# Tile 2 of the input transposed by a DMA instead of TensorE, with a new order of the first phase's steps

## Chip, cores and metric

One core of a Trainium2 chip. The metric is device time in microseconds (us) of one execution; a smaller number is better. Engines are named as in the profile: PE is TensorE's matmul stream, PEld its weight loads, DVE VectorE, ACT ScalarE, POOL GpSimd, SP the engine that issues most DMAs.

## What is computed

The input x has 2048 rows of 512 (bf16). It is layer-normalised, then goes through a linear-attention block and a gated feed-forward block, whose results are added to x.

```python
xn  = layernorm(x)                                   # no weight, no bias
qkv = xn @ wqkv                                      # 32 heads of 16
pq, pk = phi(q), phi(k)                              # phi(t) = (t+1 if t>0 else exp(t)) + 1e-6
kv  = einsum("bhsd,bhse->bhde", pk, v); z = pk.sum(over rows)
o   = einsum("bhqd,bhde->bhqe", pq, kv) / (einsum("bhqd,bhd->bhq", pq, z) + 1e-6)
out = x + o @ wo + (silu(xn @ w_gate) * (xn @ w_up)) @ w_down      # feed-forward width 1792
```

## The kernel before, in words

The rows are cut into 16 tiles of 128. The kernel has three stages. **Phase 1** (to about 48.7 us of the span) loads x, normalises each tile, transposes it, multiplies it with the query and key columns of wqkv, applies phi, and accumulates G = xn^T pk over all tiles in four PSUM banks. The middle stage makes the gate and up products of the feed-forward block (for rows from 384 on with a seven-product scheme for 2x2 blocks). The last stage makes the down projection and adds the attention part. All engines run their own instruction streams, in order; a small planner (`_Program`, line 63) puts a semaphore wait in front of each instruction that reads or overwrites something another engine has yet to finish. Nothing reorders anything: **the order of phase 1 is a hand-written list of steps** (the string given to `run`, line 536), and each engine executes its own steps in that order.

A step is a letter and a tile number. Those that matter here, with the engine and the line of their code:

- `S`: mean and variance of a tile, two instructions on DVE (L307, L310). `M`: minus the mean of tile 1, on ACT (L334).
- `R`: 1/standard deviation, two small ACT instructions (L314, L316). `r`: three more small ones for tiles 0 and 1 (L321 to L323); `o`: two small POOL instructions that use them (L326, L329).
- `a`, `b`, `C`: tiles 0 and 1, which are only centred before the product (DVE, L339, L349). `L`: normalise a tile on DVE (L377); `P`: the same on POOL, one small instruction and one large (L392, L395); `N`, `A` do it with ACT.
- `J`: the normalised copy of tile 0 or 1 that G needs, on POOL, a small and a large instruction (L369, L372).
- `c`, `d`, `W`, `X`: four 128x128 transposes of a tile on PE into a PSUM bank (L407; `c` and `d` do two each): `W` uses bank 2, `X` bank 3. `e`, `f`, `w`, `Z`: the copy of that bank to SBUF (ACT L415, DVE L417).
- `D`: the other way to transpose: one transposing DMA, issued by SP (L423).
- `K`, `k`: first and second half of the key product of a tile, `Q`, `q` those of the query product (PE, L444; two matmuls of 128x512 a half for tiles 0 to 3; from tile 4 on `k` and `q` are whole, four matmuls).
- `x`, `y`: exp of that product, ACT (L462 for tiles 0 and 1, L465). `z`: a copy of a query product out of its bank, ACT (L454), for tiles whose `u` comes much later.
- `m`, `n`: the minimum in phi, POOL (L472). `s`, `u`: the sum that gives pk or pq, DVE (L483).
- `G`: the four matmuls of a tile for G (PE, L493). `F`: filler matmuls (L297) that only keep PE busy.

A product takes the next of **four PSUM banks, 4 to 7, in turn** (`nextbank`, line 432). It may only overwrite a bank when the ACT and DVE steps (`x` and `s`, or `y` and `u`, or `y` and `z`) of the product four places earlier have read it. So a product waits for work that belongs to another tile, and the order of the products decides which.

Tiles 0 to 3 are transposed by PE, the others by `D`. The loads of x are issued first: the halves of tile 0, tiles 1 and 3, by SP, the second half of tile 0 and tile 2 by ACT; then SP issues three parts of wqkv and, in one run, tiles 4 to 15. The transposing DMAs follow on the same SP stream (first `D5`), and the loads of the feed-forward weights come behind some of them.

Of the kernel before, what the change touches and what calls it, by code (L numbers as in the profile page):

```python
# [121 lines left out]
def bass_parallel_sum__linear_attn_block__swiglu_ffn__prompt_kernel(nc, A_x, A_wqkv, A_wo, B_x, B_w_gate, B_w_up, B_w_down, out):  # L122
# [5 lines left out]
    with contextlib.ExitStack() as es:  # L128
# [401 lines left out]
        def run(text):  # L530
            late = {int(w[1:]) for w in text.split() if w[0] == "z"}
            later.update({t: i for i, t in enumerate(int(w[1:]) for w in text.split() if w[0] == "u" and int(w[1:]) in late)})
            for w in text.split():
                steps[w[0]](int(w[1:]))

        run("""
            S0 M1 a0 b0 c0 R0 d0 F2 C1 S3 e0 N0 W1 r0 K0 o0 f0 R3 w1 S2 K1 P3 k0 S1 R2 J0 W3 x0 k1 Q1 L2 R1 w3
            m0 X2 q1 r1 Z2 Q3 s0 x1 o1 q3 S5 y1 K3 m1 k3 R5 n1 s1 G0 z1 L5 J1 x3 S9 K2 D5 Q0 z3 m3 S4 k2 R9 q0
            y3 P9 s3 G1 x2 S8 R4 m2 D9 Q2 z0 q2 P4 s2 R8 k5 z2 L8 n3 D4 S15 q5 x5 y0 S12 m5 G2 D8 y5 s5 q9 y2
            n5 S10 R15 k9 n0 y9 u5 R12 n9 k4 x9 L15 u9 D15 q4 m9 x4 L12 R10 s9 m4 q8 y4 D12 S11 P10 k8 z8 s4  # L540
            n4 R11 D10 G9 S13 x8 N11 A11 G5 m8 u4 y8 n2 s8 D11 G3 R13 S14 A0 P13 k15 S7 R14 k12 n8 D13 x15 L14
            S6 m15 q10 x12 D14 s15 m12 k10 y10 s12 n10 k11 x10 u10 R7 m10 q15 x11 s10 q11 m11 y15 L7 R6 s11
            D7 n15 k13 y11 u15 q13 n11 x13 L6 u11 D6 m13 q14 y13 s13 n13 q12 y14 u13 n14 k14 y12 u14 n12 q7
            x14 u12 m14 k7 y7 L1 s14 D0 D1 n7 k6 x7 u0 m7 q6 u7 x6 s7 m6 G4 y6 s6 n6 G12 u2 G14 u6 u1 G6 u8 G10
            u3 G11 G15 G8 G13 G7
        """)
        fload("sp", "wg", wg, B_w_gate, 1)
        wload("sp", 2)
# [304 lines left out]
        X1, X2 = slice(T0, T0 + TB), slice(T0 + TB, S)  # L853
# [507 lines left out]
```

## Time and profile before

| | |
|---|---|
| median of 3 runs | 199.21 us (199.07 to 199.49) |
| the profiled execution, its time | 199.49 us |
| its span from first to last instruction | 198.2 us |
| PE busy | 193.8 us (98%) |
| DVE busy | 170.6 us (86%) |
| ACT busy | 157.3 us (79%) |
| POOL busy | 127.6 us (64%) |
| granted TensorE clock | 1.00 |

A timeline row reads: start in us from the span's start, duration in us, engine, line, operation, output<-input, shape, how many instructions the row merges, and in brackets the engine's idle time just before and what ended it. PE rows end late: matmuls are pipelined, so the time that one costs is read from one start to the next, not from the duration. The same holds, by 0.1 us or less, for the other engines. A row of DMA issues gives the size and the median time from issue to landing.

### The profile page before, as it was taken

How to read it: one execution, taken by the hardware profiler on the slowest of the kernel's cores; microseconds unless marked ns; L12 is line 12 of the kernel's file. 1: busy time of each engine (PE TensorE's matmuls, PEld its weight loads, DVE VectorE, ACT ScalarE, POOL GpSimd, SP SyncE). 2: the span in 40 equal slices, each digit the busy share in tenths (PEclk: the TensorE clock that was granted, in tenths of full speed). 3: DMA queues.
4: the chain of work that ended last, by engine and by line, in shares of the span. 5: the costliest groups of instructions: out<-in, count | busy, mean ns of one | idle time of the engine just before them, and what ended most of it. 6: DMA issues, size and time to landing. Idle time of an engine off the chain costs nothing.

```text
span 198.2 us, 3561 instructions
## 1 busy us (share of the span) xinstructions
PE 193.8 (98%) x1193; PEld 115.2 (58%) x1207; DVE 170.6 (86%) x328; ACT 157.3 (79%) x314; POOL 127.6 (64%) x158
## 2 busy tenths in 40 slices
PE   8899999999999999999999999999999999999995
PEld 2344444444655555555555555555555888888884
DVE  2999998896997799887888998887888999998886
ACT  3799888699698998898999888998897967575300
POOL 3687877799999487689778877868579004413220
PEclk9999999999999999999999999999999999999999
DMA  5943248799900000111110221111000012132223
GB/s 171 360 131 81 61 86 231 211 275 373 348 14 0 3 0 0 28 26 30 28 26 2 55 53 26 26 26 31 2 0 2 3 40 66 33 77 66 45 65 121
DMA packets 28899, 15.97 MB, mean 81 GB/s; under 512 B 17232, under 2 KB 28880, under 8 KB 28880
## 3 DMA queue, kind: packets, MB, share of 16 engines
q1 hardware_dynamic: 28320, 15.28, 28.1%
q10 hardware_dynamic: 560, 0.46, 0.7%
q8 instruction: 9, 0.15, 0.3%
q14 instruction: 10, 0.08, 0.1%
HBM read 9.70 MB, written 2.10 MB: 60 GB/s over the span
## 4 chain that ended last, share of the span: by engine, by line
PE 94%; DVE 2%; DMA 2%; issue 1%; ACT 0%; POOL 0%; SPq 0%
PE pb L896 35%; PE pb L1104 16%; PE pb L444 13%; PE pb L565 9%; PE pb L493 7%; PE pb L719 6%; PE pb L1110 5%; DMA x_sb<-in_A_x_dram 2%; PE pb L723 2%; PE pb L625 0%; PE pb L711 0%; DVE pq L483 0%; PE pb L407 0%; POOL ef L472 0%; DVE stats L307 0%
## 5 line engine op out<-in xcount | busy, mean ns | idle before, releaser
L691 POOL TENSOR_TENSOR pq<-pq,rden 128x512 bf16<-128x512 bf16 x16 | 16.9, 1056 | 36.2 <-DVE rden L684 26.7
L896 PE MATMUL pb<-xnT,wgu 128*128 128x416 bf16 x112 | 26.6, 339 | 0.0
L444 PE MATMUL pb<-wqkv,xnT 128*128 128x512 bf16 x110 | 25.1, 379 | 0.2
L665 POOL TENSOR_TENSOR pz<-pq,zbc 128x512 f32<-128x512 bf16 x16 | 18.9, 1180 | 5.1 <-ACT pz L658 3.5
L565 PE MATMUL pb<-xnT,wgu 128*128 128x384 bf16 x112 | 19.9, 326 | 0.1
L931 DVE TENSOR_TENSOR pb<-p,pb 128x416 f32<-128x416 f32 x28 | 16.6, 595 | 3.6 <-PE pb L896 1.9
L472 POOL TENSOR_SCALAR ef<-ef 128x512 bf16<-128x512 bf16 x25 | 15.5, 620 | 5.8 <-ACT ef L465 5.6
L926 ACT ACTIVATE zacc<-pb,iw 128x416 bf16<-128x416 f32 x28 | 16.4, 614 | 3.1 <-PE pb L896 2.3
L444 PEld LDWEIGHTS pb<-wqkv,xnT 128*128 128x128 bf16 x112 | 10.9, 98 | 13.4 <-DVE pk L483 0.4
L936 DVE TENSOR_TENSOR c<-pb,p 128x416 f32<-128x416 f32 x28 | 16.4, 588 | 2.3 <-PE pb L896 0.3
L465 ACT ACTIVATE ef<-pb 128x512 bf16<-128x512 f32 x25 | 14.8, 593 | 3.9 <-PE pb L444 3.9
L940 POOL TENSOR_TENSOR hT<-c,zacc 128x416 bf16<-128x416 f32 x16 | 15.3, 974 | 2.3 <-ACT zacc L926 1.7
L510 POOL TENSOR_TENSOR zacc<-zacc,pk 128x512 f32<-128x512 f32 x13 | 16.0, 1232 | 1.0
L906 ACT ACTIVATE pb<-pb 128x416 f32<-128x416 f32 x28 | 13.7, 501 | 3.0 <-PE pb L896 1.9
L896 PEld LDWEIGHTS pb<-xnT,wgu 128*128 128x128 bf16 x112 | 10.9, 98 | 8.7
L921 ACT ACTIVATE zacc<-pb,iw 128x416 bf16<-128x416 f32 x28 | 15.7, 626 | 0.0
L565 PEld LDWEIGHTS pb<-xnT,wgu 128*128 128x128 bf16 x112 | 10.8, 98 | 7.0 <-DVE xn L613 0.2
L1104 PE MATMUL pb<-wgu,xnT 128*128 128x256 f16 (+1 forms) x112 | 14.9, 273 | 0.0
L896 PE MATMUL pb<-xnT,wqkv 128*128 128x416 bf16 x56 | 14.4, 339 | 0.3
L896 PE MATMUL pb<-wo,wqkv 128*128 128x416 f16 x56 | 14.4, 339 | 0.0
L896 PE MATMUL pb<-GT,wqkv 128*128 128x416 f16 x56 | 14.4, 339 | 0.0
L307 DVE BATCH_NORM_STATS2 stats<-x_sb 128x6 f32<-128x512 bf16 x16 | 10.8, 678 | 3.2 <-DMA x_sb<-in_A_x_dram 3.2
(202 smaller groups left out, 494.1 us busy)
## 6 DMA issues: line engine op xcount, KB each, us to landing
x_sb<-in_A_x_dram SPq DMA_DIRECT2D x14, 128.0 KB, 3.8
wgu<-in_B_w_gate_dram SPq DMA_DIRECT2D x2, 896.0 KB, 5.2
wgu<-in_B_w_up_dram SPq DMA_DIRECT2D x2, 896.0 KB, 8.0
wd<-in_B_w_down_dram SPq DMA_DIRECT2D x2, 896.0 KB, 13.1
out_dram<-out_sb SPq DMA_DIRECT2D x24, 64.0 KB, 1.6
wqkv<-in_A_wqkv_dram SPq DMA_DIRECT2D x3, 256.0 KB, 4.4
wqkv<-in_A_wqkv_dram SPq DMA_DIRECT2D x1, 512.0 KB, 6.3
wo<-in_A_wo_dram SPq DMA_DIRECT2D x1, 512.0 KB, 8.8
```

What stands on the lines that cost most here:

```text
L444: K.add("pe", [(lambda e, c=c: e.matmul(banks[b][:, :], src[:, c, t * P:(t + 1) * P], wqkv[:, c, col:col + D], start=(c == 0), stop=(c == ...
L472: K.add("pool", lambda e: e.tensor_scalar(out=buf, in0=buf, scalar1=top, scalar2=0.0, op0=ALU.min, op1=ALU.max), r=[bkey] + tkeys, w=[bkey])
L510: K.add("pool", lambda e: e.tensor_tensor(out=dst, in0=acc, in1=more, op=ALU.add), r=[key, mkey], w=[dkey])
L565: fns.append(lambda e, c=c, b=b, w_=w_: e.matmul(banks[b][:, 0:T0], w_[:, c, fc * P:(fc + 1) * P], xnT[:, c, 0:T0], start=(c == 0), stop=( ...
L665: K.add("pool", lambda e: e.tensor_tensor(out=halves(i), in0=two(pq[:, t, :]), in1=two(zbc[:, :]), op=ALU.mult), r=[("pq", t), ("zbc",)] + ...
L691: K.add("pool", lambda e: e.tensor_tensor(out=heads(pq[:, t, :]), in0=heads(pq[:, t, :]), in1=rden[:, i, :][:, :, None].broadcast_to([P, N ...
L896: K.add("pe", [(lambda e, c=c: e.matmul(banks[bank][:, 0:TS], L[i][:, c, :], R[i][:, c, ts], start=(start and c == 0), stop=(c == 1), skip ...
L921: K.add("act", lambda e: e.activation(sil4[:, q, :], bk(a), ACT.Silu, scale=iw[:, 0:1]), r=[B(a), ("iw",)], w=[("sil4", q)], a=[("zacc", 0 ...
L926: K.add("act", lambda e: e.activation(sil4[:, 2 + q, :], bk(d), ACT.Silu, scale=iw[:, 0:1]), r=[B(d), ("iw",)], w=[("sil4", 2 + q)], a=[(" ...
L931: K.add("dve", lambda e: e.tensor_tensor(out=bk(d), in0=p5[:, q, :], in1=bk(b), op=ALU.subtract), r=[B(b), ("p5", q)], w=[B(d)])
L936: K.add("dve", lambda e: e.tensor_tensor(out=c22[:, q, :], in0=bk(b), in1=p5[:, q, :], op=ALU.subtract), r=[B(b), ("p5", q)], w=[("c22", q)])
L1104: K.add("pe", [(lambda e, k=k: e.matmul(split(banks[b][:, 0:HD]), L[:, k, :], cut[:, :, k * P:(k + 1) * P], start=(start and k == 0), stop ...
```

## The change

Only the list of steps changes. `X2` and `Z2` (transposes of tile 2 on PE and their copy on DVE) are gone; `D2`, a transposing DMA, takes their place, and is the first on SP, ahead of `D5`. The order of the steps is rewritten from the start to about `G2`; from `k4` on the two lists agree.

```diff
-S0 M1 a0 b0 c0 R0 d0 F2 C1 S3 e0 N0 W1 r0 K0 o0 f0 R3 w1 S2 K1 P3 k0 S1 R2 J0 W3 x0 k1 Q1 L2 R1 w3
-m0 X2 q1 r1 Z2 Q3 s0 x1 o1 q3 S5 y1 K3 m1 k3 R5 n1 s1 G0 z1 L5 J1 x3 S9 K2 D5 Q0 z3 m3 S4 k2 R9 q0
-y3 P9 s3 G1 x2 S8 R4 m2 D9 Q2 z0 q2 P4 s2 R8 k5 z2 L8 n3 D4 S15 q5 x5 y0 S12 m5 G2 D8 y5 s5 q9 y2
-n5 S10 R15 k9 n0 y9 u5 R12 n9 k4 x9 L15 u9 D15 ...
+S0 a0 b0 M1 c0 d0 R0 F2 e0 S2 C1 f0 S3 r0 R3 W1 N0 K0 k0 S1 o0 x0 w1 P3 m0 R2 K1 W3 k1 R1 L2 J0 w3 r1 Q1
+q1 s0 o1 S5 K3 x1 z1 k3 Q3 y1 R5 q3 x3 J1 G0 m1 S9 D2 s1 y3 L5 R9 Q0 K2 S4 S8 z3 m3 k2 R4 x2 D5 P9 G1 s3
+q0 n1 R8 Q2 y0 L8 m2 D9 q2 s2 z0 z2 k5 x5 y2 D8 P4 n0 q5 D4 m5 y5 n3 S10 q9 S15 R15 k9 n5 s5 y9 S12 u5
+G2 n9 R12 L15 u9 k4 x9 D15 ...
```

By engine, the first steps are then (before, after):

```
PE    c0 d0 F2 W1 K0 K1 k0 W3 k1 Q1 X2 q1 Q3 q3 K3 k3 G0 K2 Q0 k2 q0 G1 Q2 q2 k5 q5 G2 q9 k9 | k4
      c0 d0 F2 W1 K0 k0 K1 W3 k1 Q1 q1 K3 k3 Q3 q3 G0 Q0 K2 k2 G1 q0 Q2 q2 k5 q5 q9 k9 G2    | k4
DVE   S0 a0 b0 C1 S3 f0 w1 S2 S1 L2 w3 Z2 s0 S5 s1 L5 S9 S4 s3 S8 s2 L8 S15 S12 s5 S10 u5 | L15
      S0 a0 b0 S2 C1 f0 S3 S1 w1 L2 w3 s0 S5 S9 s1 L5 S4 S8 s3 L8 s2 S10 S15 s5 S12 u5    | L15
ACT   M1 R0 e0 r0 R3 R2 x0 R1 r1 x1 y1 R5 z1 x3 z3 R9 y3 x2 R4 z0 R8 z2 x5 y0 y5 y2 | R15
      M1 R0 e0 r0 R3 x0 R2 R1 r1 x1 z1 y1 R5 x3 y3 R9 z3 R4 x2 R8 y0 z0 z2 x5 y2 y5 | R15
POOL  N0 o0 P3 J0 m0 o1 m1 n1 J1 m3 P9 m2 P4 n3 m5 n5 n0 | n9
      N0 o0 P3 m0 J0 o1 J1 m1 m3 P9 n1 m2 P4 n0 m5 n3 n5 | n9
SP    D5 D9 D4 D8 | D15
      D2 D5 D9 D8 D4 | D15
```

More of the change, by code (lines that the diff above doesn't have):

```diff
@@ L536, in bass_parallel_sum__linear_attn_block__swiglu_ffn__prompt_kernel @@
         run("""
-            S0 M1 a0 b0 c0 R0 d0 F2 C1 S3 e0 N0 W1 r0 K0 o0 f0 R3 w1 S2 K1 P3 k0 S1 R2 J0 W3 x0 k1 Q1 L2 R1 w3
-            m0 X2 q1 r1 Z2 Q3 s0 x1 o1 q3 S5 y1 K3 m1 k3 R5 n1 s1 G0 z1 L5 J1 x3 S9 K2 D5 Q0 z3 m3 S4 k2 R9 q0
-            y3 P9 s3 G1 x2 S8 R4 m2 D9 Q2 z0 q2 P4 s2 R8 k5 z2 L8 n3 D4 S15 q5 x5 y0 S12 m5 G2 D8 y5 s5 q9 y2
[L540 to L545, printed above, removed]
+            S0 a0 b0 M1 c0 d0 R0 F2 e0 S2 C1 f0 S3 r0 R3 W1 N0 K0 k0 S1 o0 x0 w1 P3 m0 R2 K1 W3 k1 R1 L2 J0 w3 r1 Q1
+            q1 s0 o1 S5 K3 x1 z1 k3 Q3 y1 R5 q3 x3 J1 G0 m1 S9 D2 s1 y3 L5 R9 Q0 K2 S4 S8 z3 m3 k2 R4 x2 D5 P9 G1 s3
+            q0 n1 R8 Q2 y0 L8 m2 D9 q2 s2 z0 z2 k5 x5 y2 D8 P4 n0 q5 D4 m5 y5 n3 S10 q9 S15 R15 k9 n5 s5 y9 S12 u5
+            G2 n9 R12 L15 u9 k4 x9 D15 q4 m9 x4 L12 R10 s9 m4 q8 y4 D12 S11 P10 k8 z8 s4 n4 R11 D10 G9 S13 x8 N11
+            A11 G5 m8 u4 y8 n2 s8 D11 G3 R13 S14 A0 P13 k15 S7 R14 k12 n8 D13 x15 L14 S6 m15 q10 x12 D14 s15 m12 k10
+            y10 s12 n10 k11 x10 u10 R7 m10 q15 x11 s10 q11 m11 y15 L7 R6 s11 D7 n15 k13 y11 u15 q13 n11 x13 L6 u11
+            D6 m13 q14 y13 s13 n13 q12 y14 u13 n14 k14 y12 u14 n12 q7 x14 u12 m14 k7 y7 L1 s14 D0 D1 n7 k6 x7 u0 m7
+            q6 u7 x6 s7 m6 G4 y6 s6 n6 G12 u2 G14 u6 u1 G6 u8 G10 u3 G11 G15 G8 G13 G7
         """)
```

## Prediction

> **What bounds the kernel now.** I read the page's busy times and its chain of work first, then the timeline of each engine over phase 1.
>
> ```profile
> PE 193.8 (98%) x1193; PEld 115.2 (58%) x1207; DVE 170.6 (86%) x328; ACT 157.3 (79%) x314; POOL 127.6 (64%) x158
> PE 94%; DVE 2%; DMA 2%; issue 1%; ACT 0%; POOL 0%; SPq 0%
> ```
>
> PE is busy for 98% of the span and is 94% of the chain that ended last. So a microsecond that PE loses anywhere moves the end by as much, and one that PE doesn't have to work is gained, as long as nothing else takes its place. PE's own rows show where it waits:
>
> ```profile
> 5.50 0.40 PE L407 MATMUL pb<-ident,hT 128*128 128x128 bf16 x4 [0.31 <-DVE hT L349]
> 5.89 0.59 PE L444 MATMUL pb<-wqkv,hT 128*128 128x512 bf16 x2
> 6.82 1.04 PE L444 MATMUL pb<-wqkv,hT 128*128 128x512 bf16 x4 [0.34 <-DVE hT L417]
> 7.83 0.40 PE L407 MATMUL pb<-ident,xn 128*128 128x128 bf16 x4
> 8.06 1.03 PE L444 MATMUL pb<-wqkv,hT 128*128 128x512 bf16 x4
> 9.00 0.40 PE L407 MATMUL pb<-ident,xn 128*128 128x128 bf16 x4
> 9.23 0.59 PE L444 MATMUL pb<-wqkv,hT 128*128 128x512 bf16 x2
> 9.66 1.95 PE L444 MATMUL pb<-wqkv,xnT 128*128 128x512 bf16 x8
> 11.45 0.81 PE L493 MATMUL pb<-pk,hT 128*128 128x512 bf16 x3
> 12.31 0.59 PE L444 MATMUL pb<-wqkv,xnT 128*128 128x512 bf16 x2
> ...
> 26.13 13.97 PE L444 MATMUL pb<-wqkv,xnT 128*128 128x512 bf16 x63
> ```
>
> These are W1; K0; K1 and k0; W3; k1 and Q1; X2; q1; Q3, q3, K3, k3; G0; K2. From start to start, two product matmuls cost 0.43 (9.23 to 9.66), four transposes 0.23 (9.00 to 9.23), the four of a G 0.86 (11.45 to 12.31). Adding these up, PE stands still for 0.50 ahead of K1 (5.89 + 0.43 = 6.32, K1 at 6.82; the row says 0.34 because the durations contain the drain of the array), 0.15 ahead of W3 and 0.08 ahead of X2. From 9.66 on it has no wait worth naming; the last row, 64 matmuls of which one is not recorded, has no bracket at all, and 64 x 0.216 = 13.8.
>
> **What is removed, and its worth.** X2's four transposes go: 0.23 of PE, which would be the whole gain, -0.1%, if nothing else moved. Z2, a copy on DVE, goes too; DVE is off the path there, so it is worth something only where PE waits for DVE. Everything else is order. PE's later work is the same, in the same order from k4 on, so the sum is: when does PE reach the same point of its work? I add up the new order with the durations of these rows:
>
> ```profile
> 4.14 0.48 DVE L339 TENSOR_SCALAR hT<-x_sb,mv 128x256 bf16<-128x256 bf16 x2
> 5.09 0.35 DVE L349 TENSOR_SCALAR hT<-x_sb,negm 128x512 bf16<-128x512 bf16 x1 [0.46 <-ACT hT L334]
> 5.36 0.69 DVE L307 BATCH_NORM_STATS2 stats<-x_sb 128x6 f32<-128x512 bf16 x1
> 6.08 0.18 DVE L310 BATCH_NORM_AGGREGATE mv<-stats 128x2 f32<-128x6 f32 x1
> 6.18 0.59 DVE L417 COPY hT<-pb 128x256 bf16<-128x256 bf16 x2
> ...
> 8.29 0.65 DVE L377 TENSOR_SCALAR xn<-x_sb,mv,rstd 128x512 bf16<-128x512 bf16 x1
> ...
> 9.78 0.74 DVE L483 SCALAR_TENSOR_TENSOR pk<-pb,flo,ef 128x512 bf16<-128x512 f32 x1
> ```
>
> ```profile
> 0.83 0.87 ACTq L227 DMA_DIRECT2D x_sb<-in_A_x_dram  x2
> ```
>
> ```profile
> x_sb<-in_A_x_dram ACTq DMA_DIRECT2D x1, 128.0 KB, 3.2
> ```
>
> **Step 1, DVE to w1.** Before: a0 and b0 (4.14), an idle 0.46 for M1, C1 (5.09), S3 (5.36), then f0 and w1 (6.18, done at 6.77), and K1 starts at 6.82. An S takes 0.82 from start to start (5.36 to 6.18), C1 0.27. Now S2 stands ahead of C1, and S3 and S1 ahead of w1. Tile 2 has landed: its load is the second of ACT's two issues, at about 1.25, and 1.25 + 3.2 = 4.45. So S2 starts at 4.52, where b0 leaves DVE, C1 at 4.52 + 0.82 = 5.34 (0.25 later than before, and W1 with it, at 5.75), f0 at 5.61. f0 copies half as much as w1, so it has about a third of the pair's 0.59 (the row of 6.18), 0.18 to the next start, and S3 starts at 5.79, **0.43 later than before**. f0 and w1 together take 0.59, and two S stand between them: w1 is done at 5.61 + 0.59 + 2 x 0.82 = 7.84. K1 can start at 7.90.
>
> PE meanwhile: W1 5.75, K0 5.98, k0 6.41 to 6.84, then it waits **1.06** for K1. K1 7.90 to 8.33, W3 8.33 (its input P3 is done at 8.20, step 2) to 8.56, k1 8.99, Q1 9.42, q1 9.85. Before, q1 ended at 9.66 with X2 done. So PE is **0.19 later**, although X2 is gone. k0, which now runs ahead of K1, fills 0.43 of the wait for w1; the rest is idle.
>
> **Step 2, POOL to s1.** These are P3 (its large part), J0 (small, large), m0, o1 (two small), m1, and the exp x0 on ACT:
>
> ```profile
> 7.01 0.76 POOL L395 TENSOR_SCALAR xn<-x_sb,nm,rstd 128x512 bf16<-128x512 bf16 x1 [0.47 <-ACT rstd L316]
> 7.74 0.19 POOL L369 TENSOR_SCALAR nmg<-mv 128x1 f32<-128x1 f32 x1
> 8.04 0.76 POOL L372 TENSOR_SCALAR hT<-x_sb,nmg,r 128x512 bf16<-128x512 bf16 x1
> 8.91 0.68 POOL L472 TENSOR_SCALAR ef<-ef,cap 128x512 bf16<-128x512 bf16 x1
> 9.68 0.19 POOL L326 TENSOR_SCALAR flo<-std 128x1 f32<-128x1 f32 x1
> 9.96 0.19 POOL L329 TENSOR_SCALAR cap<-std 128x1 f32<-128x1 f32 x1
> 10.49 0.68 POOL L472 TENSOR_SCALAR ef<-ef,cap 128x512 bf16<-128x512 bf16 x1 [0.35 <-ACT ef L462]
> ```
>
> ```profile
> 8.05 0.76 ACT L462 ACTIVATE ef<-pb,lstd,rstd 128x512 bf16<-128x512 f32 x1
> ```
>
> P3 waits for R3, which waits for S3, so all 0.43 reaches it: 7.44 to 8.20. The order behind it is now m0, J0, o1, **J1**, m1, where J1 used to come after m1. From start to start: P3 0.73 (7.01 to 7.74), m about 0.67, a J 0.30 + 0.73 = 1.03, o1 0.28 + 0.15 = 0.43. m0 8.17 (x0 follows R3 on ACT, at about 7.15, and is done at 7.91), J0 8.84, o1 9.87, J1 10.30, m1 11.33 to 12.01. Then s1 on DVE, 0.72 to 0.74 long as s0: 12.04 to 12.77. DVE itself would have been free at 11.5: L2 starts at 8.4, when R2 is ready, and lasts its 0.65 beside POOL's m0, w3 ends at about 9.3, s0 at 10.0, S5 and S9 take 1.64.
>
> Who waits for s1? The product four places after K1. The products take the banks in turn: K0 4, K1 5, Q1 6, K3 7, Q3 4, Q0 5. **Q0 can't start before s1 has read bank 5**, at 12.82. PE from 9.85: K3, k3, Q3, q3 take 4 x 0.43 to 11.57 (w3 and s0, for which K3 and Q3 wait, are done at 9.3 and 10.0), G0 to 12.43. So PE waits **0.39** for s1, where before, K2 took that bank at 12.31 and s1 was done at 12.0.
>
> **Step 3, the DMA.** D2 can be issued when L2 is done, at 9.0, but stands on SP behind the loads of x:
>
> ```profile
> 3.69 5.70 SPq L227 DMA_DIRECT2D x_sb<-in_A_x_dram  x12
> ```
>
> ```profile
> x_sb<-in_A_x_dram SPq DMA_DIRECT2D x1, 128.0 KB, 3.2
> ```
>
> ```profile
> DMA to landing us min/median/max: 2.4/2.5/5.1
> ```
>
> The twelve issues end at 9.39. The second row is the last of them, tile 15, issued at 8.94, landed at 12.1. The third is over the 14 transposing DMAs: at best D2 lands at 9.39 + 2.4 = 11.8, at worst, as the one behind a 896 KB load, at 9.39 + 5.1 = 14.5. No row has one right behind twelve loads. I take 12.5, shortly after tile 15, because these loads are smaller than that one. By the Trainium skill, DMA: Bandwidth & Descriptors, section "Two DMAs through the same engine are not ordered", descriptors of one queue start in order but are pipelined; so D2 would follow the x loads rather than overtake them, which excludes 11.8 and would give 12.1 or more, with the same sum. K2, which reads it, now stands behind Q0: 12.82 + 0.43 = 13.25. The DMA is hidden with 0.7 to spare, cover that would be gone if Q0 didn't wait (12.43 + 0.43 = 12.86, still behind 12.5). D5, D9, D8 and D4 behind it on SP each find their tile's normalisation later than SP.
>
> **Step 4, to k4.** K2, k2, G1, q0 follow to 15.41 without a wait. Q2 takes K3's bank and needs s3, which DVE reaches behind s1 (12.04, 0.65 to the next start), L5, S4 and S8. L5 takes between half of L2's 0.65 and all of it, as POOL is idle or busy beside it; then s3 starts at 12.69 + 0.33 to 0.57 + 2 x 0.82 = 14.66 to 14.90 and is done 0.69 later, at 15.35 to 15.6. PE asks at 15.41: a wait of 0 to 0.2. I take 0, and keep 0.2 for the range. Behind it k5, q5, q9, k9 and G2 have half a microsecond or more.
>
> **The sum.** At its Q0 the new order is at 12.82, where the old one was at 12.31 with the same work done: 0.19, less the 0.07 of small gaps that the old order still has up to there, plus 0.39, is **+0.50**, with X2's 0.23 already credited. Nothing later returns it, since PE has no idle time to give. The profiled execution took 199.49 and would take 199.99. It was the longest of the three; on their median, 199.21, the forecast is **199.7 us**.
>
> **Rivals.**
>
> *Only step 1 counts.* POOL's chain is all start-to-start sums, and J1 or o1 may pack closer; if m1 is done by 11.6, Q0 doesn't wait. Then +0.12: 199.3. For it: J and m have gaps in the old order, so their closest spacing isn't seen. Against: P3, m1 and J's two parts are taken from spacings without a wait.
>
> *D2 lands late.* If landing takes 5.1, K2 starts at 14.5 instead of 13.25: another 1.25, 200.95. It decides from a landing 3.9 after the issue. For it: the queue is full of x. Against: those loads are over by 12.1. That the change saves nothing, because PE then waits for the DMA longer than its transposes took, is this case too, with any landing after 13.5.
>
> *Faster: the chain through DVE.* The chain of waits leaves PE once in phase 1:
>
> ```profile
> 31.51 0.61 ACT ef L465
> ...
> 33.90 6.21 PE pb L444 x28
> ```
>
> If PE is really paced there by ACT, POOL and DVE, a delay of 0.50 at 12 us is absorbed, and DVE's saving (Z2, as large as w1, two thirds of the pair's 0.59) comes out at the end: -0.4, 198.8. It decides from 0.5 of hidden waiting in PE's 64 matmuls up to 39.9. Against it: their row holds none (64 x 0.216 = 13.8 of 13.97), and DVE's part of the list up to L15 comes out no earlier than before.
>
> **Chances and range.** Forecast 0.53, own range 199.5 to 200.0; only step 1 0.27; D2 late 0.10; faster through DVE 0.10. A measurement here can tell about 0.2%, 0.4 us, from no change; the forecast's +0.50 is close to that bound, so I give a quarter of it to "within". Slower: 0.40 of the forecast, all of D2 late, a little of step 1, 0.52. Faster: 0.09. Within: 0.39. The range 199.1 to 200.4 leaves out the faster case and the far half of D2's landing, some 0.15.
>
> **What would show it.** In the profile after: C1 at 5.34 and K1 at 7.9, with a PE bracket of about 0.9 that names L417 (step 1); J1 ahead of m1, m1 ending at 12.0, and a PE bracket of 0.2 to 0.4 at a query product at 12.8 that names L483 (step 2); D2 issued at 9.4, landed at 12 to 13, and no PE wait for a DMA (step 3); the start of the 64 matmuls at 26.6 instead of 26.13 (the sum). K1 at 7.9 without the second bracket is the first rival. A start of the 64 at or before 26.2 would say that I overrate DVE's or POOL's spacing; a late start of theirs but an end at 198.2 would be the third rival.

## The result and the profile after

| | before | after |
|---|---|---|
| median (runs) | 199.36 us (6) | 200.14 us (6) |
| lowest to highest | 199.07 to 199.55 | 199.97 to 200.31 |
| the profiled execution | 199.49 us, span 198.2 | 200.14 us, span 198.9 |

The ratio after / before is 1.0045, with a 95% interval of 1.0031 to 1.0059: slower by 0.3 to 0.6%. The forecast was 199.7 in a range of 199.1 to 200.4. The two profiled executions differ by 0.65 us, the medians by 0.78; the forecast had +0.50.

From the page of the changed kernel, its busy times and the engines' shares of the chain that ended last:

```profile
PE 194.7 (98%) x1203; PEld 115.6 (58%) x1203; DVE 170.0 (85%) x327; ACT 157.7 (79%) x314; POOL 127.7 (64%) x158
...
PE 93%; ACT 3%; DVE 1%; DMA 1%; issue 0%
```

PE still bounds the kernel. DVE's busy time fell by 0.6 us (Z2, a copy of 0.42 in the profile before, among it), and nothing came of it. The timeline of PE shows why; its columns are start, duration, operation, count, and in brackets the wait:

```profile
4.72 0.64 PE L297 MATMUL pb<-const-bfloat16-1.0 128*128 128x256 bf16 x2
...
5.97 1.26 PE L444 MATMUL pb<-wqkv,hT 128*128 128x512 bf16 x4
7.69 0.60 PE L444 MATMUL pb<-wqkv,hT 128*128 128x512 bf16 x2 [0.46 <-DVE hT L417]
...
9.65 1.89 PE L444 MATMUL pb<-wqkv,xnT 128*128 128x512 bf16 x8
11.38 1.03 PE L493 MATMUL pb<-pk,hT 128*128 128x512 bf16 x4
12.97 0.60 PE L444 MATMUL pb<-wqkv,hT 128*128 128x512 bf16 x2 [0.57 <-ACT rstd L316]
13.42 1.03 PE L444 MATMUL pb<-wqkv,xnT 128*128 128x512 bf16 x4
...
26.80 13.98 PE L444 MATMUL pb<-wqkv,xnT 128*128 128x512 bf16 x64
```

These are F2; K0 and k0; K1; K3, k3, Q3, q3; G0; Q0; K2 and k2; and the 64 matmuls. There is one large stall behind G0: G0 ends at 11.38 + 0.86 = 12.24 and Q0 starts at 12.97, so PE stands still for **0.73** (the bracket says 0.57, since durations contain the drain). At the same point of the work the old order was at 12.31, so the new one is 0.66 behind. The start of the 64 matmuls is 26.80 instead of 26.13, 0.67 behind. Where each later stage starts shows that, but for 0.05, nothing is given back or added:

| start, us | before | after | difference |
|---|---|---|---|
| 64 matmuls of phase 1 | 26.13 | 26.80 | 0.67 |
| gate and up products | 48.57 | 49.24 | 0.67 |
| block products | 68.82 | 69.44 | 0.62 |
| down projection | 154.51 | 155.14 | 0.63 |
| end of PE's last row | 196.13 | 196.76 | 0.63 |

So the loss is made before 13 us and carried to the end.

### The profile page after: what moved, and what is told of

Its sections match the earlier page's. It is cut to its first block, busy times and chain, and to the rows that moved or that the text cites. A ratio compares the mean times of both kernels' runs of the same rounds, so it can differ in the third digit from the quotient of the medians.

```text
span 198.9 us, 3568 instructions
## 1 busy us (share of the span) xinstructions
PE 194.7 (98%) x1203; PEld 115.6 (58%) x1203; DVE 170.0 (85%) x327; ACT 157.7 (79%) x314; POOL 127.7 (64%) x158
## 4 chain that ended last, share of the span: by engine, by line
PE 93%; ACT 3%; DVE 1%; DMA 1%; issue 0%
PE pb L895 35%; PE pb L1103 16%; PE pb L444 12%; PE pb L564 9%; PE pb L493 7%; PE pb L718 6%; PE pb L1109 5%; PE pb L722 2%; DMA x_sb<-in_A_x_dram 1%; ACT ef L462 1%; DVE stats L307 1%; PE pb L624 0%; PE pb L710 0%; ACT rstd L316 0%; ACT lnv L314 0%; ACT pq L462 0%
## 5 line engine op out<-in xcount | busy, mean ns | idle before, releaser
L1109 PE MATMUL pb<-M,pk 128*128 128x256 bf16 x96 | 13.6, 273 | 0.0
```

The source lines that it names most:

```text
L1109: K.add("pe", [(lambda e, g=g: e.matmul(dk(b), pk[:, SLOT[t], g * P:(g + 1) * P], M[:, g, lo:lo + HD], start=False, stop=(g == NG - 1), sk ...
```

## Experiments

**Theory:** the loss is the stall at Q0, which waits for s1 at the end of POOL's chain (P3, m0, J0, o1, J1, m1); the DMA is hidden, but only because K2 now stands behind Q0. **Rivals:** the loss is PE's wait for K1 (step 1 alone); the DMA itself costs the time wherever it is read; something else that the new list moves early (S2, S1 or k0) sets the start of POOL's chain. In the diffs below the list of steps is cut to the words around the edit. Beside each result stands the kernel before as it ran together with it, in three sets. The DMA alone, K2 moved back, m1 ahead of J1 and w1 ahead of S1 share one (199.17); K2 and y0 moved, and the early DVE steps, the second (199.56); the last two kernels the third (199.26).

### The DMA alone, in the old order

```diff
-L2 R1 w3 m0 X2 q1 r1 Z2 Q3
+L2 D2 R1 w3 m0 q1 r1 Q3
```

> The kernel before with one part of the change only: X2 and Z2 out, D2 in, first on SP; every other step stays where it was, K2 right behind G0. Theory A (the loss comes from the order: w1 behind S2 and S1, and m1 behind J1): DVE and POOL are as before, so Q0's bank is free in time and K1 starts at 6.8; PE reaches K2 at 12.31 - 0.23 = 12.1, but D2, issued at 9.4, lands 3.4 later as in the changed kernel, at 12.8, so PE waits 0.7 for the DMA and the 64 matmuls start 0.5 later than before: 199.36 + 0.5 = 199.9. Theory B (the transposing DMA is what costs, wherever K2 stands): as the changed kernel, 200.1, with the wait on the DMA. Theory C (the DMA costs nothing and would have landed in time anywhere): 199.36 - 0.23 = 199.1. The trace tells A from B by the PE wait: its size and its place.

Measured: 200.19 us (199.91 to 200.64, 6 runs), before 199.17; ratio 1.0049 [1.0031, 1.0067]. PE's row of K2, and D2's issue with its time to landing:

```profile
12.84 0.59 PE L444 MATMUL pb<-wqkv,xnT 128*128 128x512 bf16 x2 [0.66 <-DVE stats L307]
```

```profile
9.42 1.30 SPq L423 DMA_TRANSPOSE xnT<-xn  x1
```

```profile
xnT<-xn SPq DMA_TRANSPOSE x1, 3.3
```

D2 was issued at 9.42 and landed 3.3 later, at 12.7; K2 starts at 12.84, behind a bracket of 0.66. The bracket names DVE's S, whose result K2 doesn't read. Of the things that K2 does wait for, s1 had left its bank at 11.80, so the landing is the one that fits. In the old order K2 stands at 12.31, so the DMA costs more than the transposes that it saves. The 64 matmuls start at 26.65, 0.52 behind. So the DMA is no gain without moving K2, and the new order around Q0 and K2 is not an ornament.

### The DMA with K2 moved back

```diff
-S9 K2 D5 Q0 z3 m3 S4 k2 R9 q0 y3
+S9 Q0 D5 q0 z3 m3 S4 K2 R9 k2 y3
-D4 S15 q5 x5 y0 S12
+D4 S15 y0 q5 x5 S12
```

This is the kernel of the run before with these lines changed too.

> As the run with the DMA alone, but K2 and k2 stand behind Q0 and q0 (0.86 of PE work), and y0 moves ahead of q5, since Q0 and K2 change banks. Theory A: Q0 reads a bank that s1 has left at about 11.9, PE reaches it at 12.1 and K2 at 12.95, just after the landing at 12.8: no wait, and X2's 0.23 is gained: the 64 matmuls start at 25.9 instead of 26.13, 199.36 - 0.23 = 199.1. Theory B (the DMA costs wherever K2 stands): slower than before, 199.7 or more.

Measured: 200.27 us (199.78 to 200.73, 8 runs), before 199.17; ratio 1.0047 [1.0031, 1.0062]. Rows of PE (W3, Q0 with q0, K2 with k2, Q2 with q2, q5), and the one of ACT that q5 waits for:

```profile
7.37 0.40 PE L407 MATMUL pb<-ident,xn 128*128 128x128 bf16 x4
...
11.72 1.03 PE L444 MATMUL pb<-wqkv,hT 128*128 128x512 bf16 x4
12.82 1.02 PE L444 MATMUL pb<-wqkv,xnT 128*128 128x512 bf16 x4
...
14.54 1.89 PE L444 MATMUL pb<-wqkv,xnT 128*128 128x512 bf16 x8
17.00 1.04 PE L444 MATMUL pb<-wqkv,xnT 128*128 128x512 bf16 x4 [0.57 <-ACT pq L462]
```

```profile
16.18 0.77 ACT L462 ACTIVATE pq<-pb,lstd,rstd 128x512 bf16<-128x512 f32 x1
```

D2 is nearly hidden: it landed at 9.43 + 3.3 = 12.7, and K2 starts 0.24 after Q0 and q0 are through (11.72 + 0.86 = 12.58). PE reaches Q2 at 14.54, where before had it at 14.90, but these 0.36 are no gain of the transposes: this execution was already 0.46 ahead at W3 (7.37 against 7.83). From W3 to Q2 it took 7.17, before 7.07 in both of its profiles (the second has W3 at 7.34 and Q2 at 14.41).

y0 ends at 16.95, and q5 starts at 17.00. The expected 199.1 was missed through my own edit: with Q0 and q0 ahead of K2 the turns of the banks changed, q5 needs the bank that y0 reads, and on ACT y0 came only one place earlier.

### The DMA with K2 and y0 moved

```diff
-S9 K2 D5 Q0 z3 m3 S4 k2 R9 q0 y3 P9 s3 G1
+S9 Q0 D5 q0 z3 m3 S4 K2 R9 k2 y3 y0 P9 s3 G1
-q5 x5 y0 S12
+q5 x5 S12
```

This is the kernel with the DMA alone, with these lines changed too.

> The run with K2 behind Q0 and q0 once more, with y0 moved up on ACT (behind y3) instead of standing behind z2. In that run PE reached Q2 at 14.54, 0.36 ahead of the kernel before, and then waited 0.57 for y0, whose bank q5 takes. Theory A: with y0 at 13.6 that wait is gone, D2 is hidden (K2 at 12.8 to 13.0), and the gain of X2's removal is seen: the 64 matmuls start at 25.8 to 25.95 instead of 26.13, and the time is 0.2 to 0.3 below before, 199.17 - 0.25 = 198.9. Theory B (a transposing DMA costs wherever its reader stands): not faster than before.

Measured: 199.29 us (199.15 to 200.05, 12 runs), before 199.56 (198.84 to 201.19, 23 runs); ratio 0.9996 [0.9975, 1.0017]: the same as before. Rows of PE from Q3 on, and of DVE's s0:

```profile
9.15 2.13 PE L444 MATMUL pb<-wqkv,xnT 128*128 128x512 bf16 x8
11.11 1.03 PE L493 MATMUL pb<-pk,hT 128*128 128x512 bf16 x4
11.97 1.03 PE L444 MATMUL pb<-wqkv,hT 128*128 128x512 bf16 x4
12.84 1.02 PE L444 MATMUL pb<-wqkv,xnT 128*128 128x512 bf16 x4
...
20.11 3.61 PE L444 MATMUL pb<-wqkv,xnT 128*128 128x512 bf16 x16 [0.20 <-DMA xnT<-xn]
```

```profile
9.43 0.75 DVE L483 SCALAR_TENSOR_TENSOR pk<-pb,flo,ef 128x512 bf16<-128x512 f32 x1 [0.36 <-POOL ef L472]
```

No wait for D2 is left: Q0, q0 from 11.97 and K2, k2 from 12.84 run without a gap. But the 0.23 of X2 is gone again. The eight matmuls from 9.15 take 1.96 to the start of G0, where eight cost 8 x 0.216 = 1.73: K3 waits for s0, s0 for POOL's m0. X2 used to run inside that wait. From W3 (7.62) to Q2 (14.57) PE takes 6.95, 0.12 less than before's 7.07. That is lost again at k4, which waits for tile 4's transposing DMA: from 18.02 to 20.11 are 2.09 for eight matmuls, 0.36 too much (0.20 in the bracket). The 64 matmuls start at 26.16, before's 26.13. So of the 0.23 nothing reaches PE's later work in this list. That no list could keep a part of it isn't shown: the wait at k4 is not one for D2, and the interval of the times alone, 0.9975 to 1.0017, leaves room for a gain of 0.1%.

### m1 ahead of J1, in the changed kernel

```diff
-x3 J1 G0 m1 S9
+x3 G0 m1 J1 S9
```

> The changed kernel with one step moved: m1 ahead of J1 on POOL, as it was before the change. Theory A: m1 starts at 10.4 instead of 11.45 and s1 at 11.5, where S9 leaves DVE, so it is done at 12.25; PE reaches Q0 at 12.24 to 12.4 and its 0.57 wait shrinks to 0.1 or less. Gain 0.5: 200.14 - 0.5 = 199.65; the K1 wait stays at 0.46. Theory D (the wait for w1 ahead of K1 makes the loss by itself, and the one at Q0 is only an effect of it): no gain, 200.1.

Measured: 199.75 us (199.38 to 200.23, 12 runs), before 199.17; ratio 1.0026 [1.0014, 1.0037]. Of PE, the rows of G0, Q0 and K2; of POOL, m1; of DVE, s1:

```profile
11.46 1.03 PE L493 MATMUL pb<-pk,hT 128*128 128x512 bf16 x4
12.33 0.60 PE L444 MATMUL pb<-wqkv,hT 128*128 128x512 bf16 x2
13.00 1.04 PE L444 MATMUL pb<-wqkv,xnT 128*128 128x512 bf16 x4
```

```profile
10.67 0.69 POOL L472 TENSOR_SCALAR ef<-ef,cap 128x512 bf16<-128x512 bf16 x1 [0.17 <-ACT hT L454]
```

```profile
11.55 0.72 DVE L483 SCALAR_TENSOR_TENSOR pk<-pb,flo,ef 128x512 bf16<-128x512 f32 x1
```

m1 starts at 10.67, before J1, s1 is done at 12.27, and Q0 follows G0 with no wait: 11.46 + 0.86 = 12.32. The profiled time falls by 0.44 from 200.14, the median by 0.39 (and by 0.44 against the next run, w1 ahead of S1, which keeps J1 ahead of m1 and ran in the same set), the start of the 64 matmuls by 0.41 to 26.39. The place of one step thus holds about half of the loss. The stall was 0.73 and only 0.4 comes back, because the next bound is close: K2 starts at 13.00, 0.24 after Q0's 0.43 (12.76), as D2 landed at 9.42 + 3.5 = 12.9. The 64 matmuls start 0.26 behind before's, and these 0.24 are nearly all of that. The wait ahead of K1 is as long as in the changed kernel (0.49 against 0.46), so what came back didn't come from there.

### w1 ahead of S1, in the changed kernel

```diff
-K0 k0 S1 o0 x0 w1 P3
+K0 k0 o0 x0 w1 S1 P3
```

> The changed kernel with one step moved: w1 ahead of S1 on DVE. Theory A: K1 starts at 7.1 instead of 7.69, when k0 is through, but W3 still waits for P3 (done 8.04), so W3 moves by 0.05 at most, and Q0 still waits for s1 behind POOL's chain, which this doesn't touch: no change, 200.14 within 0.1, and the wait moves from K1 to W3. Theory D (the wait for w1 makes the loss): the 0.46 comes back, 199.7.

Measured: 200.19 us (200.04 to 200.55, 6 runs), before 199.17; ratio 1.0047 [1.0032, 1.0063]. No gain over the changed kernel. PE's rows of k0 with K1, and of Q0:

```profile
6.80 1.02 PE L444 MATMUL pb<-wqkv,hT 128*128 128x512 bf16 x4 [0.58 <-DVE hT L417]
...
13.12 0.60 PE L444 MATMUL pb<-wqkv,hT 128*128 128x512 bf16 x2 [0.84 <-ACT rstd L316]
```

The wait ahead of K1 has gone and K1 is done half a microsecond earlier, yet Q0 starts 0.15 later than in the changed kernel, because s1 is no earlier. That ends the first rival: K1's wait alone doesn't decide. It also shows a bound that I hadn't in my chain. k0 itself waits to 6.80, and not for w1, which it doesn't read, but for the part of wqkv that it multiplies with, which landed at 6.7 (the table of the next section).

### The early DVE steps put back, in the changed kernel

```diff
-e0 S2 C1 f0 S3 r0 R3 W1 N0 K0 k0 S1 o0 x0 w1 P3
+e0 C1 S3 f0 r0 R3 W1 N0 K0 k0 o0 x0 w1 S2 S1 P3
```

> The changed kernel with DVE's first steps in the order of before (C1, S3, f0, w1, S2, S1); POOL, ACT, PE stay in the changed order, J1 ahead of m1. Theory A: the wait ahead of K1 (0.46) goes, P3 starts 0.4 earlier, and POOL's chain to s1 starts with it, from m0 at 7.9 to 8.0 instead of 8.15 since x0 follows k0; s1 is done at 12.5 to 12.7 instead of 12.92 and PE asks for its bank at 12.0, so the wait at Q0 stays 0.5 to 0.7: gain 0.3, 200.19 - 0.3 = 199.9. Theory D (w1's delay is the loss and the wait at Q0 follows from it): both waits go, gain 1.0, at or below before. Theory E (k0 ahead of K1 makes x0, and so POOL's chain, hang on the landing of a part of wqkv): the start of x0 follows k0, k0 starts 0.05 after that landing, and Q0's wait is as large as in the changed kernel or larger.

Measured: 200.24 us (200.01 to 201.22, 12 runs), before 199.56; ratio 1.0039 [1.0018, 1.0059]. No gain. P3 starts at 6.77 here, 0.51 earlier than in the changed kernel, and it helps nothing. PE's rows of k0 with K1, and of Q0; the part of wqkv that k0 reads, with its time from issue (at 2.19) to landing:

```profile
7.23 1.02 PE L444 MATMUL pb<-wqkv,hT 128*128 128x512 bf16 x4 [0.80 <-DVE stats L307]
...
13.56 0.60 PE L444 MATMUL pb<-wqkv,hT 128*128 128x512 bf16 x2 [0.84 <-ACT rstd L316]
```

```profile
wqkv<-in_A_wqkv_dram SPq DMA_DIRECT2D x1, 256.0 KB, 4.9
```

The part landed at 2.19 + 4.9 = 7.1, k0 ran at 7.23, and all of POOL's chain came later with it. The four profiles that share this order of POOL's steps, sorted by that landing (P3 is the large part):

| us | landing | k0's weights | x0 starts | P3 starts | m0 | m1 | s1 ends | Q0 |
|---|---|---|---|---|---|---|---|---|
| changed kernel, again | 6.1 | 6.22 | 7.00 | 7.28 | 8.02 | 11.31 | 12.78 | 12.84 |
| changed kernel | 6.4 | 6.44 | 7.27 | 7.28 | 8.15 | 11.45 | 12.92 | 12.97 |
| w1 ahead of S1 | 6.7 | 6.77 | 7.43 | 7.09 | 8.30 | 11.60 | 13.06 | 13.12 |
| early DVE steps back | 7.1 | 7.20 | 7.86 | 6.77 | 8.73 | 12.03 | 13.50 | 13.56 |

From m0 to m1 it is 3.29 or 3.30 every time, and Q0 follows s1's end by 0.05 or 0.06. So m0 sets Q0. And m0 starts when the later of P3 and x0 is done: 0.74 after P3's start in the first row, as my step 2 had it, and 0.87 or 0.88 after x0's start in the other three, where P3 is done first. In these three P3 gets earlier from row to row while Q0 gets later. There **x0 starts the chain**, and x0 needs k0. In the last two rows k0 ran right behind that landing: x0 starts 0.66 after the load of k0's weights. In the changed kernel it starts 0.83 after it, so there the landing isn't what held it; step 2 below shows what did. With 0.66 and 0.87, a landing from about 6.4 on makes x0 later than a P3 that starts at 7.28 (an estimate from these rows: 8.02 - 0.87 - 0.66 = 6.49 for the weights), and from there on no DVE step at the start is worth anything. In the old list K1 runs ahead of k0, so that k0's place in before's profile, 7.25, covers a landing up to then.

### Both kernels once more

> The kernel before, unchanged, for a second profile. It shows how far the start varies between executions (first x tile, landings of wqkv, the first matmul at full rate), since forecast and sums hang on one profile. Theory A: the waits are the same few (ahead of W1 and K1) and the 64 matmuls start within 0.2 of 26.13. Theory F (the difference between the kernels comes from such variation at the start): they start anywhere up to 26.8.

> The changed kernel, unchanged, for a second profile. Theory A: again a wait of 0.4 to 0.5 ahead of K1 and of 0.4 to 0.8 ahead of Q0, the latter ending 0.05 after s1, and the 64 matmuls start at 26.6 to 26.95. Theory F (variation at the start): the waits change from one execution to the next and the start of the 64 matmuls lies anywhere from 26.1.

One profile each: before 199.4 us, span 198.2; after 199.99, span 198.7. In the second profile of the changed kernel, PE's rows of K1 and of Q0 show the same two waits:

```profile
7.68 0.61 PE L444 MATMUL pb<-wqkv,hT 128*128 128x512 bf16 x2 [0.84 <-DVE hT L417]
...
12.84 0.60 PE L444 MATMUL pb<-wqkv,hT 128*128 128x512 bf16 x2 [0.44 <-DVE pk L483]
```

Here the landing was early (6.1), m0 followed P3 as forecast, and Q0's 12.84 and the 64 matmuls' 26.66 are within 0.06 of the forecast's 12.82 and 26.6. That it is so close is luck: P3 started 0.16 before the forecast's 7.44, and the chain behind it took about as much longer than added up (step 2 below). The stall at Q0 names DVE's pk, s1, where the first profile named ACT's rstd. G0 ends at 11.37 + 0.86 = 12.23, so PE stands still for 0.61.

Before's second profile reaches the 64 matmuls at 25.64, 0.49 ahead of its first, and ends PE's work only 0.07 earlier (196.06 against 196.13). Its gate and up stage took 20.66 instead of 20.25. The row of ACT in which that stage begins to differ, in the second profile:

```profile
51.80 0.95 ACT L749 ACTIVATE p<-wgu 128x896 bf16<-128x896 bf16 x1 [2.05 <-DMA wgu<-in_B_w_up_dram]
```

In both profiles ACT waits for the second half of the up weights until about the same time, 51.80 here and 51.88 in the first, which idled 1.64 before it. So an earlier phase 1 meets a load that is no earlier. That suggested that time won in phase 1 can be lost to this load, which the next run tries.

### The up weights loaded earlier

The kernel before, with the load of the second half of the up weights put ahead of two others:

```diff
-        wload("sp", 2)
-        woload("sp")
         fload("sp", "wu", wu, B_w_up, 1)
+        wload("sp", 2)
+        woload("sp")
```

> The kernel before, with one load moved on SP: the second half of the up weights (896 KB) ahead of the value columns of wqkv and of wo (1 MB together). Theory G (a floor behind phase 1): in the second profile of before, phase 1 ended 0.49 earlier than in the first (48.08 instead of 48.57) and the end came no earlier, because the stage behind it waited on ACT for that load, which lands at 51.7 in both. By G the load lands about 2.5 to 3 earlier now, ACT's wait of 1.6 to 2.0 goes, and the stage from the first gate product to the first block product takes 20.20 always; the time falls by 0.1 to 0.3 in the median, because the executions with an early phase 1 keep their lead. Against G (the 0.46 in that one execution was chance): ACT's wait goes or shrinks, the time stays as before.

Measured: 199.20 us (199.08 to 199.68, 11 runs), before 199.26 (15 runs); ratio 0.9999 [0.9990, 1.0008]. ACT's wait for the load is gone, its step starts at 50.16, and the stage takes 20.20, which is 0.05 less; the time is the same. So in the timed runs this load takes nothing that can be seen. That it took 0.41 in the one early execution is what that profile shows; no timed difference bears on it.

### D4 earlier as well

The kernel with K2 and y0 moved and the up weights early, and P4 put ahead of m2:

```diff
-R4 m2 D9 Q2 z0 q2 P4 s2
+R4 P4 m2 D9 Q2 z0 q2 s2
```

> The run with K2 behind q0 and y0 early, plus two mendings: P4 ahead of m2 on POOL, so that D4 is issued 0.3 earlier (k4 waited 0.20 for its landing), and the load of the up weights as in the run before this one. Theories A and G together: D2 hidden, X2's 0.23 gained less the 0.2 that K3 now waits for s0, the wait ahead of k4 gone: the 64 matmuls start at 25.9 to 26.0, the stage behind takes 20.20, and the time is 0.2 to 0.4 below before. Theory B (the DMA instead of PE's transposes brings nothing): not faster than the run with the load alone.

Measured: 200.56 us (200.42 to 201.06, 5 runs), before 199.26; ratio 1.0073 [1.0058, 1.0089]. A miss, and a clear one. A row each of POOL (P4) and DVE (s2):

```profile
15.99 0.77 POOL L395 TENSOR_SCALAR xn<-x_sb,nm,rstd 128x512 bf16<-128x512 bf16 x1 [1.24 <-ACT rstd L316]
```

```profile
17.37 0.69 DVE L483 SCALAR_TENSOR_TENSOR pk<-pb,ef 128x512 bf16<-128x512 f32 x1 [2.10 <-POOL ef L472]
```

P4 waits 1.24 on POOL for R4 and holds m2 behind it; DVE then idles 2.10 ahead of s2. K2 also waits 0.77, since in this execution D2 landed late. The issue rows of D2 and of tile 15's load, issued just ahead of it:

```profile
xnT<-xn SPq DMA_TRANSPOSE x1, 4.2
```

```profile
x_sb<-in_A_x_dram SPq DMA_DIRECT2D x1, 128.0 KB, 4.2
```

D2 was issued at 9.42 and landed at 13.6: the rival "D2 lands late" exists, in this execution. No version here beats the kernel before.

## Why the prediction was right, point by point

The sign, the place and the mechanism came out; the size was 0.50 where the profiles show 0.65. The step that was mis-sized is **step 2: PE waits 0.39 for s1**. It was 0.73, and 0.61 in the second profile. The term behind it is POOL's chain, from the start of P3 to the end of s1: 5.33 in the forecast (7.44 to 12.77), 5.64 and 5.50 in the two profiles. The result lies in the stated range of 199.1 to 200.4, and outside the forecast's own 199.5 to 200.0.

**Step 1** held. This execution begins 0.16 earlier than before's: the pair a0, b0 starts at 3.98 against 4.14. Rows of DVE in the changed kernel:

```profile
3.98 0.48 DVE L339 TENSOR_SCALAR hT<-x_sb,mv 128x256 bf16<-128x256 bf16 x2
...
7.24 0.39 DVE L417 COPY hT<-pb 128x512 bf16<-128x512 bf16 x1
...
12.17 0.75 DVE L483 SCALAR_TENSOR_TENSOR pk<-pb,flo,ef 128x512 bf16<-128x512 f32 x1 [0.59 <-POOL ef L472]
```

w1 is done at 7.63 (forecast 7.84) and K1 starts at 7.69 (7.90); q1 ends at 9.65 (9.85). With the 0.16 added the forecast's 0.19 is 0.15. The idle time ahead of K1 was forecast as 1.06. From K0's start to K1's there are 7.69 - 5.97 = 1.72, 0.86 more than K0 and k0 should take; not all of that is idle, since K0's first matmul took 0.43 instead of 0.22 here (step 2). The bracket of "about 0.9 naming L417" came as 0.46 in one profile and as 0.84 in the other.

**Step 2** is where the size went. POOL in the changed kernel (P3, m0, J0 small and large, the first of o1's two, J1's large part, m1), then x0 on ACT, k0's weight loads, and the last three of PE's matmuls of K0 and k0:

```profile
7.28 0.76 POOL L395 TENSOR_SCALAR xn<-x_sb,nm,rstd 128x512 bf16<-128x512 bf16 x1 [0.48 <-ACT rstd L316]
8.15 0.69 POOL L472 TENSOR_SCALAR ef<-ef,cap 128x512 bf16<-128x512 bf16 x1
8.80 0.22 POOL L369 TENSOR_SCALAR nmg<-mv 128x1 f32<-128x1 f32 x1
9.13 0.76 POOL L372 TENSOR_SCALAR hT<-x_sb,nmg,r 128x512 bf16<-128x512 bf16 x1
9.98 0.19 POOL L326 TENSOR_SCALAR flo<-std 128x1 f32<-128x1 f32 x1
...
10.70 0.76 POOL L372 TENSOR_SCALAR hT<-x_sb,nmg,r 128x512 bf16<-128x512 bf16 x1
11.45 0.68 POOL L472 TENSOR_SCALAR ef<-ef,cap 128x512 bf16<-128x512 bf16 x1
```

```profile
7.27 0.78 ACT L462 ACTIVATE ef<-pb,lstd,rstd 128x512 bf16<-128x512 f32 x1 [0.18 <-PE pb L444]
```

```profile
6.44 0.29 PEld L444 LDWEIGHTS pb<-wqkv,hT 128*128 128x128 bf16 x2 [0.32 <-DVE stats L307]
```

```profile
6.40 0.83 PE L444 MATMUL pb<-wqkv,hT 128*128 128x512 bf16 x3
```

P3 is 0.16 early like the rest (7.28, forecast 7.44), s1's end 0.15 late (12.92, forecast 12.77): the chain itself is **0.31 longer** than I added up. About half (0.14) is m0: P3 to m0 took 0.87 and not 0.73, because x0 was done at 7.27 + 0.78 = 8.05, not before P3's end. I had set x0 behind R3 on ACT; its bracket says that ACT waited for PE, that is for k0. k0's weights were loaded at 6.44, right behind the landing at 2.19 + 4.2 = 6.39 (the bracket of that load names DVE's stats, which k0 doesn't read), but k0 started only at 6.64: K0's first matmul had run at half speed, from 5.97 to 6.40, and its second ran from 6.40 to 6.64. With 0.66 from the weights to x0, as in the two rows with later landings, x0 would have started at 7.10 (an estimate), and m0 would have followed P3 at 8.02. The second profile bears this out: there K0 started at 5.80 and ran at full speed, m0 started at 8.02, and Q0 came 0.13 earlier. So by these rows it was PE's late full speed that cost the 0.14 in this execution; in the runs with landings of 6.6 and more (m1 ahead of J1, w1 ahead of S1, early DVE steps back) it was the landing.

The other half is POOL's spacing: J0 small to o1 took 1.18 where I had 0.30 + 0.73 (9.13 to 9.98 is 0.85, and 0.84 or 0.85 in every run of this order, while J1 to m1 takes 0.74 or 0.75). Before's row of J0, which I quoted, had 8.04 to 8.91 = 0.87; there m0 follows x0's start (8.05) by 0.86, as in the table, so that excess was a wait, and the spacing that the new order meets wasn't to be read from it. Why the step from a J to o1 is longer, no run here isolates. The remaining 0.02 is spread over the other steps.

So s1 was late by 0.15 and PE early by 0.19 (G0 done at 12.24, forecast 12.43), and the stall came to 0.73, but its end, 12.97 against 12.82, only to 0.15 more. That is the missing 0.15 of the sum: +0.65 for +0.50. Where the wait ends counts, not how long it is.

**Step 3** held. The issue of D2, and its time to landing:

```profile
9.44 1.30 SPq L423 DMA_TRANSPOSE xnT<-xn  x1
```

```profile
xnT<-xn SPq DMA_TRANSPOSE x1, 3.4
```

It landed at 12.84 (forecast 12.5) and K2 started at 13.42 (13.25), straight behind Q0. The spare was 0.58, not 0.7, and it is made of Q0's stall: with the stall taken away (m1 ahead of J1) K2 waited 0.24. In all nine profiles with D2 it took as long to land as tile 15's load ahead of it, to 0.1 (3.3 to 4.2), and so landed about half a microsecond behind it. With the Trainium skill's rule in DMA: Bandwidth & Descriptors, section "Two DMAs through the same engine are not ordered", that the descriptors of one queue of one engine start in order, these traces agree.

**Step 4** held: Q2 started at 15.57, s3 was done at 15.43, and no wait stood between.

**The rivals.** "Only step 1 counts" is out: Q0 waits in both profiles, and m1 ahead of J1 returns 0.4. "D2 lands late" didn't happen in the changed kernel's two profiles; a landing of 4.2 in another kernel shows that it can. "Faster through DVE" is out: stage lengths behind the 64 matmuls are the same to 0.05, so PE hides no wait for DVE there.

**Profiles and medians.** 0.65 against 0.78. Before's profiled execution, 199.49, lay near the top of its 199.07 to 199.55, and the landings at the start vary from run to run (the table above spans 6.1 to 7.1). I take the remaining 0.13 for this spread; it wasn't isolated. The spread also bounds what the 0.65 can say: the 64 matmuls start at 26.13 and 25.64 in before's two profiles and at 26.80 and 26.66 in the changed kernel's, so the difference is anything from 0.53 to 1.16 by the pair that one takes. What shows step 2's error is the length of the chain inside each profile, not the 0.65.

## What to carry to other kernels

When steps are reordered, follow each moved product's inputs back to a landing, not only to the engine that last held it up: here the wait for w1 and K1 had covered the landing of a part of wqkv, and with k0 ahead of them m0, which sets Q0, starts anywhere from 8.02 to 8.73 in four profiles. A saving on the bounding engine is worth something only if the engine has work ready in its place: four transposes were 0.23 of PE, and the version that removed them with no wait for their DMA gained nothing: a part came back as a wait for s0, and the rest went into the wait for another tile's DMA. Whoever moves a product past another moves the turns of the banks too, and each step that frees a bank has to move with it. And a lead that one execution has is compared from the same earlier point in both: 0.36 at Q2 looked like a gain and was a start that was 0.46 earlier.

## What the runs showed of the hardware that was not expected

PE's full speed begins at different moments in executions of the same warm-up. The two filler matmuls F2 in before's profile, and the first matmul of K0 in the changed kernel's:

```profile
4.81 0.38 PE L297 MATMUL pb<-const-bfloat16-1.0 128*128 128x256 bf16 x2
```

```profile
5.97 0.61 PE L444 MATMUL pb<-wqkv,hT 128*128 128x512 bf16 x1
```

F2 takes 0.38 in before and 0.64 after, and K0's first matmul still takes 0.61 with its drain, where F2's pair together took 0.38: full speed by about 4.8 in the one, after 6 in the other, with the same eight matmuls ahead (0.84 to 4.4). From start to start K0's first matmul took 0.43, its second 0.24. In the run with K2 and y0 moved, the last of the eight (at 3.67) already took 0.38 with its drain, so full speed had begun by then. The Trainium skill, TensorE: Matmul & The Clock Gate, section "Part 1: The HAM clock gate", has half speed until a free-running window of about 3.4 us was busy, so that the moment differs from run to run; the traces agree in kind. It wasn't free: by step 2 it put x0, and with it Q0, about 0.13 later in the changed kernel's first profile than in its second.
